# Two feed-forward sums opened early, one pair projected in four array tiles, and feed-forward units at equal distances, in a fused attention and feed-forward kernel

## The chip, the cores and the metric

One core of a Trainium2 chip (trn2). The metric is the device time of one execution in microseconds (us). The kernel before takes 306.46 us (median of 3 runs, 306.44 to 306.5). A profile has a span a little shorter than the run's time.

## The reference

Attention over 4 batches, 8 heads, 768 positions and 64 dimensions, in which a query sees only the keys whose six hash bits equal its own; then a feed-forward layer with a SiLU gate.

```python
q_bits = (einsum('bhsd,dk->bhsk', q, proj) > 0)           # the same for k
mask   = bucket(q_bits)[..., :, None] == bucket(k_bits)[..., None, :]
scores = where(mask, q @ k.T / sqrt(D), -1e9)
x = softmax(scores) @ v                                   # -> [3072, 512]
h = x @ w_in                                              # [3072, 2048]
out = (h / (1 + exp(-h))) @ w_out                         # [3072, 512]
```

## The kernel before

Two heads make a pair, two pairs are mostly prepared together. A pair's q and k are transposed (on TensorE for the first pairs, by stream transposes on VectorE for the later ones), projected on TensorE to hash bits, compared on VectorE, and the bits are copied beside the transposed q and k, so that one matmul gives score and mask together. The program is one list of 288 steps. A step is the value products of step w, then the score product and the exponential of step w + 3. What has to be ready later is planned for a step; feed-forward units are taken from a queue between steps.

```python
def t_unit(p, i):                       # four transposes into one PSUM bank, one copy out
    tp = ps.tile([P, 512], F32, tag="m", name="tp_ps", bufs=3)
    ...
    nc.vector.tensor_copy(out=qk32[p][:, 512 * i : 512 * (i + 1)], in_=tp)      # L187

def proj_unit(*pairs):
    for c0, w in ((0, 512), (512, S - 512)):
        bp = ps.tile([P, 512], F32, tag="m", name="bp_ps", bufs=3)
        for i, p in enumerate(pairs):
            for n in range(2):                        # q, k: one 32-column tile each
                c = 32 * (2 * i + n)
                nc.tensor.matmul(bp[c : c + 32, 0:w], pw[:, 0:32],              # L279
                                 qk32[p][:, n * S + c0 : n * S + c0 + w], ...)
    ...  # two comparisons on VectorE, L285

def bits_unit(pairs, i, par):           # two copies of 13 x 768 for each head
    for n in range(2):
        if n == 1 and par == 1:
            nc.vector.tensor_scalar(...)                                        # L307
        else:
            nc.vector.tensor_copy(out=dst, in_=bits[pairs][r, :])               # L310

def mm1(ci, grp):                       # one first or second sum of the feed-forward layer
    hp = ps.tile([P, f, n], F32, tag="m", name="h_ps", bufs=3)
    for j in range(f):
        for dt in range(NDT):                         # four K tiles, one for each pair
            nc.tensor.matmul(hp[:, j, :], w_in16[...], xT[4 * b + dt][...], ...)  # L423
    nc.scalar.activation(out=th, in_=hp, func=AF.Tanh, scale=0.5)               # L427
    after.append(...)                   # VectorE's gate from th and hp, L429

for w in range(NW):                     # cut: the planned work, the queue's filling
    flush()                             # gates of the step before
    for fn in at.pop(w, []): fn()
    n = -(-(len(moeq) - keep) // left) if len(moeq) > keep else 0
    skip = w % 3 == 2 or w % QST in (20, 21)          # no unit here
    ...
    for _ in range(n): moeq.popleft()()
    av(w)                                             # value products, L365
    score(w + LEAD)                                   # score product L333, exponential L336
```

All of `tp_ps`, `bp_ps`, `xt_ps` and `h_ps` rotate through the same three PSUM banks (tag "m").

The softmax here doesn't subtract the row's maximum and nothing guards it: scores larger than these inputs give would overflow.

## Time and profile before

| | before |
|---|---|
| time, median of 3 | 306.46 us |
| span of the profile | 304.1 us |
| TensorE, ScalarE, VectorE, GpSimd busy | 99%, 69%, 59%, 42% |
| first step to step 78 | ScalarE and TensorE near balance, units not yet begun |
| step 78 to about 135, and from 145 on | TensorE with almost no gaps (the largest 0.28 us) |

TensorE's busy share hides its waits, because its rows overlap (a unit's row is 1.03 us long, and the next row starts 0.86 us after it). The distance from one start to the next is what to read; the prediction does that with the lines it shows.

### The profile page before, as it was taken

Reading aid. Unit: us, or ns where it says so; the run is one execution under the profiler, and the core shown is the slowest. Engines: PE = TensorE matmul, PEld = TensorE weight load, DVE = VectorE, ACT = ScalarE, POOL = GpSimd, SP = SyncE. Lnnn points to the kernel's source line nnn. Section 1 sums busy time; section 2 is a strip of 40 time slices with the busy share of each in tenths; the row PEclk is TensorE's granted clock in tenths of the full one; section 3 lists DMA queues with packets and bytes.
Section 4 is the critical chain, followed back from the end, with each engine's and each line's share of the span. In section 5 each row is a group of like instructions: output and inputs, shape, how many; then the busy total and the mean of one; then the engine's idle time right before and its main releaser. Section 6 shows DMA issues by size and latency. Waiting matters only on the chain.

```text
span 304.1 us, 7165 instructions
## 1 busy us (share of the span) xinstructions
PE 299.6 (99%) x2710; PEld 174.9 (58%) x2710; DVE 180.7 (59%) x341; ACT 210.7 (69%) x392; POOL 129.2 (42%) x203
## 2 busy tenths in 40 slices
PE   8999999999999999999999999999999999999996
PEld 3675855555666545555565665555566654446653
DVE  5697977799559344854696334853543442664332
ACT  5987989988877696978976766878877732442300
POOL 7589999377506851855148321765111100000000
PEclk9999999999999999999999999999999999999999
DMA  7999898999979838854068246011022013001112
GB/s 204 242 241 195 179 149 127 226 160 99 165 133 187 137 77 237 127 113 133 2 115 125 76 63 197 5 42 32 2 60 63 0 38 95 34 2 69 37 63 75
DMA packets 102786, 32.87 MB, mean 108 GB/s; under 512 B 90656, under 2 KB 99808, under 8 KB 102752
## 3 DMA queue, kind: packets, MB, share of 16 engines
q1 hardware_dynamic: 98368, 28.22, 44.6%
q0 software_dynamic: 4224, 4.19, 9.1%
q8 instruction: 21, 0.34, 0.5%
q14 instruction: 13, 0.11, 0.1%
q10 hardware_dynamic: 160, 0.00, 0.0%
HBM read 27.27 MB, written 6.29 MB: 110 GB/s over the span
## 4 chain that ended last, share of the span: by engine, by line
PE 95%; DVE 3%; ACT 1%; issue 0%; POOL 0%; ACTq 0%; POOLq 0%
PE h_ps L423 26%; PE o_ps L455 26%; PE s_ps L333 20%; PE o_ps L365 13%; PE bp_ps L279 3%; PE tp_ps L185 2%; PE o_ps L441 1%; PE warm_ps L125 1%; DVE g L429 1%; DVE qka L310 1%; ACT u L336 1%; PE bp_ps L225 1%; PE tp_ps L198 1%; PE o_ps L356 0%; DVE bits L285 0%
## 5 line engine op out<-in xcount | busy, mean ns | idle before, releaser
L336 ACT ACTIVATE u<-s_ps 128x512 f16<-128x512 f32 x288 | 156.4, 602 | 39.9 <-PE s_ps L333 39.4
L429 DVE SCALAR_TENSOR_TENSOR g<-th,h_ps 128x512 f16<-128x512 f32 x96 | 65.1, 683 | 75.4 <-ACT th L427 75.4
L423 PE MATMUL h_ps<-xT,win 128*128 128x512 f16 (+1 forms) x512 | 97.4, 325 | 0.1
L365 PEld LDWEIGHTS <-u 128*128 128x128 f16 x1152 | 67.6, 98 | 42.9 <-ACT u L336 11.2
L455 PE MATMUL o_ps<-wout,g 128*128 128x512 f16 x368 | 91.6, 379 | 0.0
L365 PE MATMUL o_ps<-vv,u 128*128 128x65 f16 x1152 | 82.8, 194 | 0.3
L427 ACT ACTIVATE th<-h_ps 128x512 f32<-128x512 f32 x96 | 57.3, 597 | 36.6 <-PE h_ps L423 33.5
L423 PEld LDWEIGHTS <-win 128*128 128x128 f16 x512 | 49.9, 98 | 31.8 <-issue 0.4
L385 POOL TENSOR_TENSOR x_pr<-osum,rec 128x384 f16<-128x384 f32 x23 | 19.0, 826 | 89.4 <-DVE rec L384 89.0
L455 PEld LDWEIGHTS <-g 128*128 128x128 f16 x368 | 35.8, 98 | 34.1
L333 PE MATMUL s_ps<-qka 71*128 71x512 f16 x192 | 52.7, 327 | 0.2 <-DVE qka L238 0.2
L333 PE MATMUL s_ps<-qkb 128*128 128x512 f16 x192 | 52.8, 326 | 0.0
L251 POOL TENSOR_SCALAR qka<-qk 64x1536 f16<-64x1536 f32 x15 | 22.0, 1465 | 12.1 <-DVE qk L246 6.8
L460 DVE TENSOR_SCALAR osb<-o_ps 128x512 f32<-128x512 f32 x23 | 15.8, 686 | 15.5 <-PE o_ps L455 15.5
L251 POOL TENSOR_SCALAR qkb<-qk 64x1536 f16<-64x1536 f32 x15 | 22.1, 1471 | 1.2
L262 POOL TENSOR_TENSOR vsa<-v_sb 128x192 f32<-128x192 f32 x32 | 19.3, 604 | 0.0
L260 POOL CAST vv<-v_sb 128x384 f16<-128x384 f32 x32 | 16.7, 520 | 0.9 <-DMA v_sb<-in_v_dram 0.5
L333 PEld LDWEIGHTS <-qka 71*128 71x128 f16 x192 | 15.4, 97 | 0.8 <-ACT qka L238 0.6
L246 DVE STREAM_TRANSPOSE qk<-k_blk 128x768 f32<-128x768 f32 x10 | 15.8, 1576 | 0.0
L246 DVE STREAM_TRANSPOSE qk<-q_blk 128x768 f32<-128x768 f32 x10 | 15.7, 1572 | 0.0
L333 PEld LDWEIGHTS <-qkb 128*128 128x128 f16 x192 | 15.4, 97 | 0.0
L379 DVE TENSOR_TENSOR osum<-o_ps,vsum 128x390 f32<-128x390 f32 x23 | 13.0, 565 | 2.3
(64 smaller groups left out, 164.8 us busy)
## 6 DMA issues: line engine op xcount, KB each, us to landing
out_dram<-osb SPq DMA_DIRECT2D x23, 256.0 KB
v_sb<-in_v_dram SPq DMA_DIRECT2D x15, 384.0 KB
q_blk<-in_q_dram SPq DMA_DIRECT2D x40, 96.0 KB
k_blk<-in_k_dram SPq DMA_DIRECT2D x40, 96.0 KB
win<-in_moe_w_in_dram POOLq DMA_DIRECT2D x4, 512.0 KB, 8.1
wout<-in_moe_w_out_dram POOLq DMA_DIRECT2D x4, 512.0 KB, 8.1
q_sb<-in_q_dram SPq DMA_DIRECT2D x5, 384.0 KB
k_sb<-in_k_dram SPq DMA_DIRECT2D x5, 384.0 KB
```

The lines of the kernel that those rows point to most:

```text
L246: nc.vector.transpose(out=dst, in_=qk_sb[p, "qk"[n]])
L251: nc.gpsimd.tensor_scalar(out=dst[rows, :], in0=qk32[p][rows, :], scalar1=CS, scalar2=1.0, op0=ALU.mult, op1=ALU.mult)
L260: nc.gpsimd.tensor_copy(out=vv[:, :, 0:D], in_=src)
L262: nc.gpsimd.tensor_tensor(out=sa, in0=src[:, 0:3], in1=src[:, 3:6], op=ALU.add)
L333: nc.tensor.matmul(sp[:, o0 : o0 + n], t[rows, S + jt * P : S + (jt + 1) * P], t[rows, c0 : c0 + n], start=True, stop=True)
L336: nc.scalar.activation(out=u, in_=sp, func=AF.Exp, scale=ESC)
L365: nc.tensor.matmul(o_ps[h][:, c0 // P + i, :], u[:, o0 + i * P : o0 + (i + 1) * P], vv[:, jt, :], start=(not direct(h) and w % NU == 0 and ...
L385: (nc.vector if direct(h) else nc.gpsimd).tensor_tensor(out=x_pr[p][:, :, par * D : (par + 1) * D], in0=o[:, 0:NJ, 0:D], in1=rec[:, :, Non ...
L423: nc.tensor.matmul(hp[:, j, :], w_in16[:, dt, ft * P : (ft + 1) * P], xT[4 * b + dt][:, c0 : c0 + n], start=(dt == 0), stop=(dt == NDT - 1))
L427: nc.scalar.activation(out=th, in_=hp, func=AF.Tanh, scale=0.5)
L429: after.append(lambda: nc.vector.scalar_tensor_tensor(out=g[ci][:, grp * f : (grp + 1) * f, :], in0=th, scalar=1.0, in1=hp, op0=ALU.add, o ...
L455: nc.tensor.matmul(o2[tt], g[ci][:, ft, ct * P : (ct + 1) * P], w_out16[:, ft, :], start=(ft == 0), stop=(ft == NFT - 1))
```

## The change

Its intent is to fill TensorE's waits before step 78, to shorten one projection that blocks ScalarE, and to stretch batch 0's feed-forward units so that they don't run dry. Its core:

```diff
+    def proj_halves(p):                       # pair 1: four tiles of 384 columns
+        for c in range(4):
+            half, n = divmod(c, 2)
+            nc.tensor.matmul(bp[32 * c : 32 * c + 32, 0:HS], pw[:, 0:32],
+                             qk32[p][:, x0 : x0 + HS], start=True, stop=True)
+        nc.vector.tensor_scalar(...)          # one comparison of 128 x 384
+    def bits_halves(p, par):                  # four copies of 13 x 384 for each head
+        for c in range(4): ...
-    plan(10, lambda: proj_unit(1))
+    plan(10, lambda: proj_halves(1))
-        plan(11 + i, lambda i=i: bits_unit((1,), 0, i))
+        plan(11 + i, lambda i=i: bits_halves(1, i))
@@ the opened sums
+        if b == 0:
+            head = slice(0, NDT - 1)          # three of four K tiles
+            first = [mm1(0, 0, head), mm1(0, 1, head)] + [closing tiles] + first[2:]
+    for i in range(2):
+        plan(66 + 4 * i, first_units[0].pop(0))
-        plan(w0 + 20, lambda Q=Q: proj_unit(2 * Q, 2 * Q + 1))
+        wp = w0 + (24 if Q == 2 else 20)      # pairs 4 and 5: step 60, not 56
@@ equal distances
+        if BST + 5 <= w < 2 * BST:            # steps 77 to 143
+            skip = w * 36 // 66 == (w - 1) * 36 // 66
```

(The list of closures is written short here, and the lines that let `mm1` keep a sum open are left out; the cast of the 16-bit identity also moved from step 50 to the start.)

## The prediction

> **What bounds the kernel now.** I read the page first, then busy time by stretches of 10 us, then the waits of ScalarE, then the timelines of ScalarE and TensorE. I count the attention in steps: a step is four value products (128x65, line 365) followed by the score product of three steps later (128x512, or two of 128x256, line 333) and one exponential (line 336). There are 288 steps. Feed-forward units are inserted between steps: a unit is four 512-column matmuls, and batch 0 has 16 first sums, 8 second sums (these 24 have a tanh, line 427) and 12 output units in its list.
>
> ```profile
> PE 299.6 (99%) x2710; PEld 174.9 (58%) x2710; DVE 180.7 (59%) x341; ACT 210.7 (69%) x392; POOL 129.2 (42%) x203
> ...
> PE 95%; DVE 3%; ACT 1%; issue 0%; POOL 0%; ACTq 0%; POOLq 0%
> ```
>
> TensorE looks full, but matmul rows overlap each other, so 99% hides short waits. I therefore took the distance from one start to the next in TensorE's timeline. It is rigid: a unit 0.86 us, four value products 0.12, a score 0.22, a pair of projections (x16) 1.43. So a step costs TensorE 0.34 us; more than that is a wait. Two stretches of steps without units, then the start of the units:
>
> ```profile
> 48.73 0.30 PE L365 MATMUL o_ps<-vv,u 128*128 128x65 f16 x4
> 48.87 0.38 PE L333 MATMUL s_ps<-qkb 128*128 128x512 f16 x1
> 49.23 0.29 PE L365 MATMUL o_ps<-vv,u 128*128 128x65 f16 x4
> ...
> 53.50 1.03 PE L423 MATMUL h_ps<-xT,win 128*128 128x512 f16 x4
> 54.36 0.28 PE L365 MATMUL o_ps<-vv,u 128*128 128x65 f16 x4
> 54.48 0.38 PE L333 MATMUL s_ps<-qkb 128*128 128x512 f16 x1
> 54.70 1.03 PE L423 MATMUL h_ps<-xT,win 128*128 128x512 f16 x4
> ...
> 108.45 0.30 PE L365 MATMUL o_ps<-vv,u 128*128 128x65 f16 x4
> 108.58 0.38 PE L333 MATMUL s_ps<-qkb 128*128 128x256 f16 x2
> 108.94 0.30 PE L365 MATMUL o_ps<-vv,u 128*128 128x65 f16 x4
> ```
>
> Near 49 us a step takes 0.49-0.50 us, not 0.34: ScalarE's exponentials set the pace (28 in 14.39 us and 22 in 10.93 us, so 0.50-0.51 each). From 53.5 us (step 78) units follow with no gap: TensorE is the bound. Near 108 us a step takes 0.49 again: batch 0's list has run dry before the next one may start. From 113 us to the end I find no gap over 0.1 us. So only waits before 113 us can be removed. ScalarE's own stalls show the other thing to remove:
>
> ```profile
> 10.85 4.86 ACT L336 ACTIVATE u<-s_ps 128x512 f16<-128x512 f32 x9 [0.37 <-PE s_ps L333]
> 16.98 9.54 ACT L336 ACTIVATE u<-s_ps 128x512 f16<-128x512 f32 x18 [1.27 <-PE s_ps L333]
> 28.17 14.39 ACT L336 ACTIVATE u<-s_ps 128x512 f16<-128x512 f32 x28 [1.65 <-PE s_ps L333]
> 43.63 10.93 ACT L336 ACTIVATE u<-s_ps 128x512 f16<-128x512 f32 x22 [1.08 <-PE s_ps L333]
> ```
>
> Each stall of over 1 us is a projection on TensorE. Three scores stand ahead of ScalarE; the stall is about the inserted work less 0.47 us (1.43 gives 0.96, measured 1.08; a 0.33 us transposition gives none, and none is there).
>
> **What the Trainium skill says.** "TensorEngine Tiling (Array Packing)", Key Properties: tiles operate independently, so matmuls of different tiles run in parallel. The trace agrees: four fp32 matmuls of pair 1 in two tiles and eight of two pairs in four tiles both take 1.43 us. "Perfetto Trace Analysis", Identifying the Most-Contended Engine: matmul busy share is not a measure of distance from the limit; here 99% with some 5 us of gaps agrees. "SBUF — State Buffer", Who interferes with whom: a VectorE instruction in a two-port mode and GpSimd block each other for a whole instruction. The trace agrees: a masking of bits (13x768, line 307) takes 0.41 us at 29.69 us, and 1.54 at 18.61, beside a GpSimd cast that began at 18.48 and took 1.47.
>
> **Part 1, pair 1 in four tiles.**
>
> ```profile
> 14.94 1.49 PE L279 MATMUL bp_ps<-qk,pw 128*32 128x512 f32 x8
> 15.40 0.12 PEld L279 LDWEIGHTS bp_ps<-qk,pw 128*32 128x32 f32 x2 [0.31 <-issue]
> ```
>
> Before, each of two tiles passes 512 + 256 columns: 1.43 us. After, four tiles pass 384 each: half, 0.72 us (the first pair does just this on line 225, at 0.78 and 0.87 us with a wait behind). Saved: 0.7 us. From 10 to 25 us TensorE has next to no gaps, and ScalarE's 18 exponentials there run at 0.53, TensorE's pace; so the 0.7 us lies on the path, and the 1.27 us stall becomes about 0.6. On VectorE one comparison of 128x384 (0.68, line 228) replaces two (1.25), but eight copies replace four. Pair 1's first bits were ready at 18.20 us and used at 19.04; both move earlier alike. Gain **0.7 us**.
>
> **Part 2, the opened sums.** Three quarters of two units, 2 x 0.65 us of matmuls, move to steps 66 and 70, where TensorE waits about 0.15 us a step; the closing quarters (0.22 us each) come at steps 77 and 79. This is not simply 1.3 us gained: by step 81 both kernels have done the same matmuls, exponentials and two tanhs, and ScalarE is the bound there. By its chain: the exponential of step 80 began at 54.06 us. Earlier by 0.7 and later by two new stalls of 0.65 - 0.47 = 0.18, exponential 79 ends at 53.72. Then tanh, exponential 80 at 0.49 each end at 54.70; adding 0.16 for the signal and 0.34 for the step, step 81 begins on TensorE at 55.20. Before it began at 56.24. The difference is 1.04, of which 0.7 is part 1's: gain **0.34 us**. Moving the projection of pairs 4 and 5 from step 56 to 60 moves its stall, and lets the transposed input of pair 2 be ready for step 66; the cast of the identity to the start fills an idle VectorE. Nothing for either.
>
> **Part 3, equal distances.** Before, units went at two of three steps from 78 and were used up at about step 135. Ten steps remained at ScalarE's pace: the gaps from 107.99 to 112.07 us add to 1.26, with smaller ones about 1.3. After, 36 units over 66 steps, 0.55 a step, last to step 143. TensorE then needs 0.34 + 0.55 x 0.86 = 0.81 us a step; ScalarE, while every unit has a tanh, 0.49 x 1.55 = 0.76, later 0.6. TensorE stays the bound by a hair. Gain **1.3 us**. It is also where I expect a small loss: the rule no longer leaves out the steps beside the projection at step 92.
>
> Sum: 0.7 + 0.34 + 1.3 = 2.3 us. **Predicted 304.1 us**, 0.8% less.
>
> **Rivals.**
> (a) VectorE becomes the bound between steps 81 and 103. It was busy 9.83 of the 10 us from 60 to 70:
>
> ```profile
> 60.00:70.00 10.00, 10.00 (x95) 5.03 (x92) 9.83 (x17) 8.50 (x17) 8.35 (x8) 1.00 0.92 143
> ```
>
> Its four stream transposes (1.57 us each) are tied to steps 77 to 87, which now pass sooner; with gates and sums it has 10.1 us of work from step 81 to 92 and TensorE only 8.9. Its lag holds banks of the three-buffer tile, so units wait. Against: units 1.5 us apart leave slack of one or two banks. It would take back 0.3 to 1.2 us: 304.4 to 305.3.
> (b) The opened sums stall ScalarE more than 0.18 each, or the first closings wait for pair 3's input: part 2 gives zero, 304.4, or costs 0.5.
> (c) Everything before 53 us is late because of data: the DMA engines are nearly full there, so an earlier schedule meets the same landing times. Against: no wait of TensorE in the profile ends with a transfer after the start. It would eat part 1: 304.8.
> (d) The opened sums fill all 1.3 us and the stage after keeps the lead: 303.2. Against: ScalarE's chain above.
> (e) The smoothing merely moves the wait: unit against ScalarE at 0.81 to 0.76 leaves TensorE waiting at each step. Then part 3 gives half, 304.7.
>
> **Range and chances.** The parts are independent and each is bounded by a wait seen in the trace: at most 0.7, 1.3 and 1.5, so 303 is the floor. Rivals a and e are the likeliest losses, about 1 us together. Range 303.2 to 305.3. Two per cent is 6.1 us, more than all waits before 113 us: faster 0.01, within 2% 0.98, slower 0.01.
>
> **What would show it.** Right: the projection of pair 1 about 0.72 us from start to next start, ScalarE's stall behind it about 0.6; steps 66 and 70 with x3 matmuls of line 456 and ScalarE stalls under 0.3; the full third unit starting near 55.2 us; steps 135 to 144 without waits and with units; from step 155 on the same timeline, 2.3 us earlier. Wrong: TensorE waits over 0.2 us ahead of first sums between 56 and 78 us (rival a), or a step time near ScalarE's pace there (e), or waits for loads before 50 us (c), or a changed length of the stretch from step 155 to the end.

## The result, and the profile after

| | before | after |
|---|---|---|
| time, median of 4 | 306.45 us (305.86 to 306.5) | 305.72 us (305.5 to 306.25) |
| ratio after to before | | 0.9983 (95%: 0.9965 to 1.0001) |
| span of the profile | 304.1 us | 304.5 us |
| first score product starts at | 8.00 us | 8.82 us |
| score product issued in step 0 starts at | 9.20 us | 10.02 us |
| the one issued in step 145, counted from there | 104.57 us | 104.14 us |

A ratio is the mean time of one kernel's fast runs over that of the other's fast runs of the same rounds, so it is not quite the ratio of the medians. The time fell by about 0.7 us of the predicted 2.4 and lies outside the range; the interval of the ratio includes 1, so by time alone even this much is not certain.

The two profiles start 0.8 us apart, in code that neither kernel changed there, so I compare by a **ledger**: the start of the score product issued in a step, counted from the one issued in step 0. From step 145 to the end all kernels take the same time, within the span's rounding to 0.1 us. The ledger comes from one profile of each kernel. Where two kernels have the same code it agrees closely: at step 50 e2, e8, e9 and e11 stand between -0.33 and -0.36 us against the kernel before. By the ledger the change gains 0.43 us. The chain that ended last shows where it went; the first line is the page's busy line, the second the chain by engine.

```profile
PE 298.0 (98%) x2710; PEld 175.2 (58%) x2710; DVE 182.0 (60%) x344; ACT 210.2 (69%) x392; POOL 128.8 (42%) x203
...
PE 91%; DVE 6%; ACT 1%; issue 1%; POOL 0%; DVEq 0%; ACTq 0%; POOLq 0%
```

VectorE's share of the chain doubled, from 3% to 6%. TensorE's timeline after the change shows two new waits, in brackets at the end of a line, and the opened sums:

```profile
15.76 0.86 PE L298 MATMUL bp_ps<-qk,pw 128*32 128x384 f32 x8
16.55 0.30 PE L393 MATMUL o_ps<-vv,u 128*128 128x65 f16 x4
...
21.67 0.38 PE L361 MATMUL s_ps<-qka 71*128 71x512 f16 x1
23.03 0.66 PE L185 MATMUL tp_ps<-ident,q_sb 128*128 128x128 f32 x4 [0.98 <-DVE qk L187]
...
49.25 0.81 PE L456 MATMUL h_ps<-xT,win 128*128 128x512 f16 x3
49.90 0.28 PE L393 MATMUL o_ps<-vv,u 128*128 128x65 f16 x4
...
57.32 0.30 PE L393 MATMUL o_ps<-vv,u 128*128 128x65 f16 x4 [0.40 <-ACT u L364]
...
66.72 1.50 PE L279 MATMUL bp_ps<-qk,pw 128*32 128x512 f32 x16
68.82 1.02 PE L456 MATMUL h_ps<-xT,win 128*128 128x512 f16 x4 [0.60 <-DVE g L465]
```

The projection of pair 1 takes 0.79 us from start to next start (1.43 before). But at step 21 a transposition that should follow the score of 21.67 after 0.22 us starts 1.36 us after it: a wait of 1.14 us for VectorE's copy out of a PSUM bank. At step 92 a first sum waits 0.67 us (2.10 between the starts, less the projection's 1.43) for a gate on VectorE.

VectorE's timeline says why the first wait is there. After:

```profile
17.50 1.80 DVE L316 COPY qka<-bits 13x384 f16<-13x384 f16 x4
19.33 1.52 DVE L316 COPY qkb<-bits 13x384 f16<-13x384 f16 x1
20.86 0.55 DVE L313 TENSOR_SCALAR qkb<-bits,sc 13x384 f16<-13x384 f16 x1
21.43 0.55 DVE L316 COPY qkb<-bits 13x384 f16<-13x384 f16 x1
21.99 0.38 DVE L313 TENSOR_SCALAR qkb<-bits,sc 13x384 f16<-13x384 f16 x1
22.30 1.27 DVE L187 COPY qk<-tp_ps 128x512 f32<-128x512 f32 x2
```

And before:

```profile
17.46 0.74 DVE L310 COPY qka<-bits 13x768 f16<-13x768 f16 x2
18.24 0.36 DVE L310 COPY qkb<-bits 13x768 f16<-13x768 f16 x1
18.61 1.54 DVE L307 TENSOR_SCALAR qkb<-bits,sc 13x768 f16<-13x768 f16 x1
20.08 1.26 DVE L187 COPY qk<-tp_ps 128x512 f32<-128x512 f32 x2
```

Four bit copies took 2.69 us (17.46 to 20.15); eight take 4.87 (17.50 to 22.37), because a copy of half the columns is hardly shorter. The Trainium skill gives a reason: "VectorE: DVE Perf Modes", The TRN2 errata, states that VectorE pays a fixed extra time per instruction when it reads SBUF. Here a 13x768 copy takes 0.35 us at best, and a 13x384 one 0.37 at best in this profile (0.28 in e10), which agrees but does not show how much of it is fixed. The copies out of PSUM for pair 2 (line 187) stand behind them in VectorE's queue, and they free the banks for the next transpositions. The 1.52 us copy ran beside this GpSimd cast and ended 0.11 us after it; the kernel before had such a block too (1.54 us, in the lines above), without a wait on TensorE:

```profile
19.27 1.47 POOL L251 TENSOR_SCALAR qkb<-qk 64x1536 f16<-64x1536 f32 x1
```

ScalarE's stalls after, to set beside the four in the prediction:

```profile
17.16 5.87 ACT L364 ACTIVATE u<-s_ps 128x512 f16<-128x512 f32 x11 [0.64 <-PE s_ps L361]
24.12 3.78 ACT L364 ACTIVATE u<-s_ps 128x512 f16<-128x512 f32 x7 [1.08 <-PE s_ps L361]
29.55 8.76 ACT L364 ACTIVATE u<-s_ps 128x512 f16<-128x512 f32 x17 [1.65 <-PE s_ps L361]
...
47.27 3.04 ACT L364 ACTIVATE u<-s_ps 128x512 f16<-128x512 f32 x6 [1.11 <-PE s_ps L361]
50.49 2.06 ACT L364 ACTIVATE u<-s_ps 128x512 f16<-128x512 f32 x4 [0.18 <-PE s_ps L361]
52.74 3.54 ACT L364 ACTIVATE u<-s_ps 128x512 f16<-128x512 f32 x7 [0.19 <-PE s_ps L361]
```

The stall behind pair 1's projection fell from 1.27 to 0.64 as predicted. A new one of 1.08 us stands where TensorE waited at step 21, and the two of 0.18 and 0.19 are those of the opened sums.

### The profile page after: what moved, and what is told of

Read it like the earlier page. It is cut to its first block, busy times and chain, and to the rows that moved or that the text cites. A ratio compares the mean times of both kernels' runs of the same rounds, so it can differ in the third digit from the quotient of the medians.

```text
span 304.5 us, 7181 instructions
## 1 busy us (share of the span) xinstructions
PE 298.0 (98%) x2710; PEld 175.2 (58%) x2710; DVE 182.0 (60%) x344; ACT 210.2 (69%) x392; POOL 128.8 (42%) x203
## 4 chain that ended last, share of the span: by engine, by line
PE 91%; DVE 6%; ACT 1%; issue 1%; POOL 0%; DVEq 0%; ACTq 0%; POOLq 0%
PE o_ps L491 26%; PE h_ps L456 26%; PE s_ps L361 18%; PE o_ps L393 11%; PE bp_ps L279 3%; PE tp_ps L185 2%; DVE g L465 2%; PE o_ps L477 1%; ACT u L364 1%; PE warm_ps L125 1%; DVE qk L246 1%; PE bp_ps L225 1%; DVE qkb L316 1%; DVE qka L316 1%; PE tp_ps L198 1%
## 5 line engine op out<-in xcount | busy, mean ns | idle before, releaser
L463 ACT ACTIVATE th<-h_ps 128x512 f32<-128x512 f32 x96 | 58.0, 604 | 37.6 <-PE h_ps L456 34.9
```

## The experiments

Twelve kernels ran; all gave the right result, and all were timed in five rounds (the kernel before ran 11 times beside each group). "Ledger" is step 0 to step 145 against 104.57 us of the kernel before. The expectations speak instead of first score to end, which carries the span's rounding. e1 to e4 ran on one chip, e5 to e8 on a second, e9 and e10 on a third, e11 and e12 on a fourth; each ratio is against the kernel before on the same chip. No kernel is 2% faster than it, but all intervals except those of the change and of e4 lie below 1.

| kernel | pair 1 | opened sums | distances | else | median us | ratio (95%) | ledger |
|---|---|---|---|---|---|---|---|
| after | 4 tiles | yes | equal | | 305.72 | 0.9983 (0.9965-1.0001) | -0.43 |
| e1 | old | yes | equal | | 305.22 | 0.9963 (0.9949-0.9977) | -1.24 |
| e2 | 4 tiles, late copies | yes | equal | | 304.43 | 0.9945 (0.9933-0.9958) | -1.57 |
| e3 | old | no | equal | | 304.29 | 0.9940 (0.9928-0.9952) | -1.70 |
| e4 | old | yes | old | | 306.33 | 1.0005 (0.9992-1.0018) | +0.20 |
| e5 | 4 tiles | yes | equal | GpSimd cast later | 304.53 | 0.9943 (0.9927-0.9959) | -1.66 |
| e6 | as e2 | yes | equal | early transposes | 304.41 | 0.9944 (0.9930-0.9958) | -1.46 |
| e7 | as e2 | yes | equal but 92 | | 304.89 | 0.9963 (0.9948-0.9978) | -1.01 |
| e8 | as e2 | no | equal | | 304.18 | 0.9936 (0.9922-0.9950) | -2.02 |
| e9 | as e2 | yes | equal | VectorE relieved | 303.94 | 0.9927 (0.9914-0.9941) | -2.30 |
| e10 | as e2 | no | equal | cast later | 304.47 | 0.9949 (0.9936-0.9962) | -1.73 |
| e11 | as e2 | no | equal | VectorE relieved | 303.65 | 0.9916 (0.9895-0.9937) | -2.24 |
| e12 | as e2 | yes | equal | as e9, projection moved | 304.34 | 0.9933 (0.9913-0.9953) | -1.92 |

One of e9's runs was slow (309.19 us at a granted clock of 0.994) and is left out of its ratio. My theory after the first look: each part does what it was made for on TensorE, and VectorE takes it back, first through the order of its queue (steps 12 to 21), then through too much work (steps 77 to 100). The rivals: a phase effect against GpSimd, ScalarE's stalls, and the nearness of a unit to a projection.

### e1: the old projection of pair 1

```diff
-    plan(10, lambda: proj_halves(1))
+    plan(10, lambda: proj_unit(1))
-        plan(11 + i, lambda i=i: bits_halves(1, i))
+        plan(11 + i, lambda i=i: bits_unit((1,), 0, i))
```

> The changed kernel with pair 1 projected as before (two array tiles, two comparisons, four bit copies). Measured inside the profile from the first score product of step 0 to the end of the span, so that the varying start drops out: before 296.1 us, changed 295.7. Theory (the eight small bit copies keep VectorE for 4.9 us at step 11-12, pair 2's transposed data waits behind them in its queue, its PSUM buffer is not free, and TensorE waits 1.14 us at step 21): without them 0.64 us of projection comes back but the 1.14 and 0.26 us waits go, so 294.9 to 295.1, time about 0.7 us under the changed kernel. Rival (the wait at step 21 comes from the rest of the change or from the phase against GpSimd): the wait stays and the run is 0.6 us longer than the changed kernel, 296.3.

The wait at step 21 was gone, and the ledger 0.81 us shorter than with the four tiles. So part 1 as written **costs** 0.8 us: it saved 0.63, then lost 1.19 at step 21 (the wait of 1.14 and slower transpositions behind it) and 0.26 near step 46. First score to end was 294.8, just under the range I gave.

### e2: the second head's bit copies later

```diff
-        plan(11 + i, lambda i=i: bits_halves(1, i))
+        if i == 0:
+            plan(11, lambda: bits_halves(1, 0))
+    for c, wc in enumerate((13, 14, 16, 17)):
+        plan(wc, lambda c=c: bits_halves(1, 1, (c,)))
```

(`bits_halves` gets an argument that picks the copies.)

> The changed kernel with the four-tile projection kept, but the four bit copies of pair 1's second head (needed only at step 24) put one each at steps 13, 14, 16 and 17, behind pair 2's first transposed copy instead of all at step 12 ahead of it. Theory (order in VectorE's queue): the 1.14 us wait at step 21 goes, first score to end 294.3 to 294.7, 1.0 to 1.4 us under the changed kernel. Rival (VectorE has too much work there whatever the order, so the wait only moves): 295.5 or more, with a wait of about 1 us at another transposition before step 30.

The wait at step 21 is gone with all eight copies still there. VectorE's timeline shows pair 2's copies between them:

```profile
16.85 1.81 DVE L316 COPY qka<-bits 13x384 f16<-13x384 f16 x4
18.69 0.69 DVE L187 COPY qk<-tp_ps 128x512 f32<-128x512 f32 x1
19.41 0.80 DVE L316 COPY qkb<-bits 13x384 f16<-13x384 f16 x1
20.23 0.55 DVE L313 TENSOR_SCALAR qkb<-bits,sc 13x384 f16<-13x384 f16 x1
20.71 0.67 DVE L187 COPY qk<-tp_ps 128x512 f32<-128x512 f32 x1
```

The order in the queue is what mattered. Of the 0.63 us, 0.28 is lost again at step 28, where the projection of pairs 2 and 3 waits 0.66 us for such a copy (0.37 before). Part 1 then gains 0.33 (e2 against e1), not 0.7.

### e3: equal distances alone

```diff
+        if BST + 5 <= w < 2 * BST:
+            skip = w * 36 // 66 == (w - 1) * 36 // 66
```

> The kernel before with the equal distances alone (part 3). Theory: the idle of about 1.3 us at steps 135 to 144 goes, and up to 0.6 us comes back as a wait beside the projection at step 92: first score to end 296.1 - 1.3 + 0.3 to 0.6 = 295.1 to 295.4. Rival (ScalarE and TensorE are so balanced that waits move into the earlier steps): 295.8 to 296.1.

Part 3 alone gains 1.70 us, more than the change as a whole and more than expected (first score to end was 294.3). The unit beside the projection at step 92 waits only 0.15 us, and steps near the end of batch 0's list follow without a gap:

```profile
106.67 1.03 PE L455 MATMUL o_ps<-wout,g 128*128 128x512 f16 x4
107.54 0.28 PE L365 MATMUL o_ps<-vv,u 128*128 128x65 f16 x4
107.66 0.38 PE L333 MATMUL s_ps<-qkb 128*128 128x512 f16 x1
107.87 0.19 PE L360 MATMUL o_ps<-vs,dmat 128*128 128x65 f16 x1
107.90 0.29 PE L365 MATMUL o_ps<-vv,u 128*128 128x65 f16 x4
```

### e4: opened sums alone

The diff is e1's together with the equal distances taken out.

> The kernel before with the two opened sums, the moved projection of pairs 4 and 5 and the moved identity cast, but the old projection of pair 1 and the old distances (part 2 alone). Theory (ScalarE sets the pace up to step 81, so opening sums early gains only the rest): 0.2 to 0.4 us less than before, first score to end 295.7 to 295.9. Rival b (the two inserted pieces stall ScalarE as much as they save): 296.1 to 296.4. Rival d (the full 1.3 us is gained): 294.8.

Part 2 alone costs 0.20 us, by the ledger; the timed ratio, 1.0005, can't tell that from nothing. At step 81 it was 0.72 us ahead of the kernel before; by step 85 it had lost 0.94 us in one wait: a first sum behind the score of 59.55 us stood still until VectorE's gate had freed a bank, and that gate stood behind a stream transposition of 1.58 us in VectorE's queue. With the waits view of TensorE:

```profile
PE h_ps L456 <- DVE g L465: 0.8, 1, 0.8
```

Rival b of the prediction gave the right sign, but its reason (ScalarE's stalls) is not the larger part.

### e5: GpSimd's cast later

```diff
-    for i in range(2):
-        plan(8, lambda i=i: cast_unit(1, i))
-        plan(8, lambda i=i: v_unit(1, (i,)))
+    plan(8, lambda: cast_unit(1, 0))
+    for i in range(2):
+        plan(8, lambda i=i: v_unit(1, (i,)))
+    plan(8, lambda: cast_unit(1, 1))
```

> The changed kernel; only GpSimd's cast of pair 1's second head is put behind the value work of pair 1 instead of between it, so that it no longer runs while VectorE copies that head's bits (one of those copies took 1.52 us, 1.17 more than its neighbours, and ended as the cast ended). First score to end was 295.7 in the changed kernel. If the lock between the two engines is a needed part of the 1.14 us wait at step 21: the copies end about 1.1 us sooner and the wait is 0 to 0.2, 294.6 to 294.9. If the number of copies alone makes it (eight at 0.4 us): the wait stays over 0.8, 295.4 or more.

VectorE's timeline:

```profile
17.42 1.81 DVE L316 COPY qka<-bits 13x384 f16<-13x384 f16 x4
19.26 0.44 DVE L316 COPY qkb<-bits 13x384 f16<-13x384 f16 x1
19.72 0.55 DVE L313 TENSOR_SCALAR qkb<-bits,sc 13x384 f16<-13x384 f16 x1
20.28 0.39 DVE L316 COPY qkb<-bits 13x384 f16<-13x384 f16 x1
20.68 0.39 DVE L313 TENSOR_SCALAR qkb<-bits,sc 13x384 f16<-13x384 f16 x1
21.00 1.27 DVE L187 COPY qk<-tp_ps 128x512 f32<-128x512 f32 x2
```

The copy of 1.52 us takes 0.44 here, and the wait at step 21 is gone. The ledger, 0.42 shorter than e1's, now pays part of the 0.7. First score to end was 294.4, better than the range given. So the wait needed three things at once: twice the copies, the block by GpSimd, and the order. Taking away any one of them removed it.

### e6: VectorE's stream transposes earlier

```diff
-            w1 = w0 + (5, 9, 12, 15)[i]
+            w1 = w0 + ((3, 6, 9, 12) if Q == 3 else (5, 9, 12, 15))[i]
```

on top of e2.

> Experiment e2 (late copies, first score to end 294.4) with VectorE's four stream transposes of pairs 6 and 7 at steps 75, 78, 81, 84 instead of 77, 81, 84, 87. Theory (the opened sums make step 77 0.56 us later, VectorE starts its crowded stretch later and is still 0.7 us behind at step 92, where a feed-forward unit waits for the gate that frees its PSUM bank): the 0.68 us wait at step 92 goes, 293.7 to 293.9. Rival (the unit stands too near the projection, VectorE's backlog is not the cause): the wait stays, 294.3 to 294.5.

The wait at step 92 went, and two others came: 0.37 us at 60.1 and 0.41 at 72.2, together 0.78 for 0.68; first score to end was 294.6. The theory as I wrote it (a late start of the crowded stretch) fell; the rival fell too.

```profile
60.70 1.02 PE L456 MATMUL h_ps<-xT,win 128*128 128x512 f16 x4 [0.21 <-DVE g L465]
...
72.82 1.02 PE L456 MATMUL h_ps<-xT,win 128*128 128x512 f16 x4 [0.26 <-DVE g L465]
```

### e7: no unit at step 92

```diff
-            skip = w * 36 // 66 == (w - 1) * 36 // 66
+            skip = w * 36 // 66 == (w - 1) * 36 // 66 or w in (92, 93)
```

on top of e2.

> Experiment e2 with no feed-forward unit at steps 92 and 93, so that the unit that waited 0.68 us behind the projection comes at step 94. If nearness to the projection is what matters: the wait goes and nothing replaces it, 293.7 to 293.9. If VectorE is behind with its work: part of the wait comes back within a few steps, 294.1 to 294.4.

Again no wait at 92, but 0.86 us at 71.7 and 0.39 at 74.1, both ahead of a first sum; first score to end was 295.0, worse than either forecast. e6 and e7 fit a wait that is VectorE's work and only moves. Busy time by stretches (VectorE is the third engine) in the changed kernel:

```profile
61.00:65.00 4.00, 4.00 (x40) 2.36 (x39) 4.00 (x6) 4.00 (x9) 3.25 (x3) 1.00 1.25 206
65.00:69.00 4.00, 3.40 (x34) 1.43 (x32) 3.93 (x8) 2.71 (x6) 3.07 (x3) 1.00 0.86 129
69.00:73.00 4.00, 4.00 (x39) 2.27 (x38) 3.89 (x8) 3.12 (x6) 3.77 (x8) 1.00 0.75 98
```

This alone proves nothing: the same view of the kernel before reads 4.00, 3.88 and 3.86 for VectorE, with no wait of TensorE over 0.1 us in that time. Whether VectorE holds TensorE has to be tested by relieving it, which e9 does.

### e8: late copies and equal distances, no opened sums

The diff is e2's, with the opened sums and the move of the projection from step 56 to 60 taken out.

> Part 1 with late copies and part 3, without the opened sums and the moved projection. From the ledger of the first four (part 3 alone -1.70 us, part 1 with late copies -0.33, opened sums +0.45): first score to end 296.1 - 2.0 = 294.1, 0.3 under e2 and e3. If the opened sums did gain something beside part 1: 294.5 or more.

As expected, to 0.1 us: the ledger is 2.02 shorter than before. The opened sums cost 0.45 in this setting (e2 against e8), and 0.46 with the old projection (e1 against e3).

### e9: VectorE relieved

```diff
-            w1 = w0 + (5, 9, 12, 15)[i]
+            w1 = w0 + ((3, 7, 11, 15) if Q == 3 else (5, 9, 12, 15))[i]
-            plan(wp + (i if Q < 4 else 0),
+            plan(wp + ((0, 6, 12, 18)[i] if Q == 3 else i if Q < 4 else 0),
```

on top of e2.

> Experiment e2 (opened sums kept, late copies; first score to end 294.4) with VectorE's load between steps 77 and 100 thinned out: the four stream transposes of pairs 6 and 7 at steps 75, 79, 83, 87, and the bit copies of these pairs at steps 92, 98, 104 and 110 instead of 92 to 95. Theory (with the opened sums VectorE, 97 to 100% busy from 57 to 77 us, sets the pace there, and e6 and e7 could only move its wait): no wait of TensorE on a gate over 0.2 us is left, and the opened sums then give 0.1 to 0.2 us over e8: 293.7 to 294.0. Rival (the opened sums lose for another reason): the waits go but first score to end stays over 294.2, or the waits stay.

The waits view of TensorE has no VectorE gate left:

```profile
PE warm_ps L125 <- POOL warm L114: 1.0, 1, 1.0
PE o_ps L393 <- ACT u L364: 0.4, 1, 0.4
PE s_ps L361 <- DVE qka L238: 0.2, 1, 0.2
```

The unit behind the projection at step 92 now follows with no wait (1.43 us after the projection's start; 2.12 in e2), and the ledger is 0.73 shorter than e2's. This is what shows that VectorE held it. The ledger is 2.30 shorter than before. That this is nearly the predicted 2.34 is luck: e9 has two further edits, and e11 gets 2.24 without part 2.

### e10: late copies and late cast, no opened sums

The diff is e8 with e5's.

> Experiment e8 (late copies, equal distances, no opened sums; first score to end 294.0) with GpSimd's cast of pair 1's second head behind the value work as well. In e8 0.28 us of the 0.63 us of the projection is given back at the projection of pairs 2 and 3 (step 28), in e5 none there but 0.21 at step 46. If VectorE's queue is what gives it back, both together keep 0.4 to 0.63 us: 293.7 to 293.9. If not, 294.0 to 294.1 as in e8.

A miss: the projection at step 28 waited 0.92 us instead of 0.65, and the ledger is 0.29 longer than e8's. The cast did not stop blocking; it met another bit copy, which took 1.33 us at 20.48 beside a cast that began at 20.23 and took 1.47. Two remedies that each work do not add up here; likely each fitted only where the other engine then stood.

### e11: relieved, no opened sums

The diff is e9's with the opened sums and the moved projection taken out.

> Experiment e9 without the opened sums and the moved projection of pairs 4 and 5. It measures what the opened sums are worth once VectorE is relieved. If they are worth what the prediction gave them (0.34 us): first score to end 294.1, against 293.7 of e9. If the whole difference of e9 from e8 was VectorE's relief: 293.7.

The ledger is 2.24 shorter than before, against 2.30 of e9. With VectorE out of the way the opened sums are worth 0.06 us, which I can't tell from zero by time (303.65 against 303.94 on different chips). e11 has the lowest median of all.

### e12: the projection of pairs 2 and 3 at step 30

```diff
-    plan(28, lambda: proj_unit(2, 3))
+    plan(30, lambda: proj_unit(2, 3))
-        plan(29 + i, lambda i=i: bits_unit((2, 3), i // 2, i % 2))
+        plan(30 + i, lambda i=i: bits_unit((2, 3), i // 2, i % 2))
```

on top of e9.

> Experiment e9 with the projection of pairs 2 and 3 at step 30 instead of 28 and its bit copies one step later each. In e9 (as in e2, e6, e7, e8) that projection waits 0.65 us for VectorE's copy of pair 3's last transposed tile, which was made one step earlier; two more steps should cover it. Expected: wait under 0.2 us, first score to end 293.1 to 293.4, the best of all. If VectorE is the bound there too: the wait moves to the next transposition or to the bits of pair 2 (needed at step 33), 293.6 or more.

A miss as well: the wait at the projection went, and pair 2's bits came too late for the first score that needs them.

```profile
PE s_ps L361 <- DVE qka L338: 0.9, 1, 0.9
...
PE tp_ps L185 <- DVE qk L187: 0.3, 1, 0.3
```

The ledger is 0.38 longer than e9's. That projection stays where it was.

## Why the prediction was wrong

The sum was 0.7 + 0.34 + 1.3. The ledger gives, for the change as it was made: part 1 +0.81 (after against e1), part 2 +0.46 (e1 against e3), part 3 -1.70 (e3 against before), together -0.43. So part 1 missed by 1.5 us, part 2 by 0.8, and part 3 gave 0.4 more than forecast.

- **Part 1, the step that failed** is this sentence: "On VectorE one comparison of 128x384 (0.68, line 228) replaces two (1.25), but eight copies replace four. Pair 1's first bits were ready at 18.20 us and used at 19.04; both move earlier alike." It asked only whether the bits are ready for their own reader. It did not ask what stands behind the copies in VectorE's queue. The copies went from 2.69 to 4.87 us, and pair 2's copies out of PSUM, next in line, held three banks; TensorE waited 1.14 us (e1, e2, e5). TensorE's own saving was right: 0.64 us against 0.7 predicted (line 225 at 0.78 us was the better guide than half of 1.43), and ScalarE's stall 0.64 against "about 0.6".
- **Part 2, the stalls.** "two new stalls of 0.65 - 0.47 = 0.18". ScalarE's idle times were as forecast, 0.18 and 0.19, but they are not the loss. In the kernel before, exponentials start 0.48 us apart and take 0.60, so they overlap; over the stall of 0.18 the next one starts 0.82 us after the last, 0.34 later than it would. By the ledger, after against before, TensorE lost 0.28 at the first (steps 65 to 69), 0.29 at the second (69 to 73) and 0.08 more by step 77. (The chain also began at 54.06 us for an exponential that the trace has at 53.93.) With the opened sums step 81 came only 0.08 us earlier than without (e1 against e3, each from its own step 0), not 0.34.
- **Part 2, what followed** was worse and is rival (a). Doing matmuls of steps 77 to 81 earlier lets TensorE pass the stretch after it sooner, but the gates, transposes and bit copies of that stretch stay on VectorE, which is 95 to 100% busy from step 81 to step 100. It is as busy there in the kernel before, so its share alone would not have told; the likely reading is that TensorE now comes sooner to the bank that a gate has yet to free. The prediction named the 10.1 us of work against 8.9 and then charged nothing for it in the sum; "units 1.5 us apart leave slack of one or two banks" was wrong at step 92. The wait was 0.67 us, within the 0.3 to 1.2 given to that rival, and the sign named for it (over 0.2 us ahead of a first sum between 56 and 78 us) came. e9 against e2 shows the cause.
- **Part 3** was right in mechanism and too small: 1.70 instead of 1.3. In e3 the gaps at steps 135 to 144 are gone, and so is the wait of 0.24 us ahead of a first sum at 74.47 us in the kernel before, which the prediction left out. The two together are 1.5 to 1.6. e3 also gains 0.15 us by step 81, where its first unit comes a step earlier, and loses 0.14 beside the projection at step 92, the small loss that was expected; the last 0.1 I can't assign.
- **Rival (c)**, late data: the waits view shows no wait of TensorE that a transfer ends, in any run. **Rival (e)**, units against ScalarE: TensorE waited 0.57 us for an exponential once, at step 80, where ScalarE's chain had said it would, and not at each step. **Rival (d)** did not happen.
- **The range** rested on the phrase "The parts are independent". They were not: parts 1 and 2 both end at VectorE. With its queue reordered and its work moved apart, the three parts reach -2.30 (e9), of which part 2 is 0.06 (e11).

What stays open: the 0.26 us lost near step 46 in the changed kernel (a transposition waits for VectorE there, and two copies took 1.58 and 1.53 us; no experiment isolated it).

## What to carry to other kernels

When work on the bounding engine is shortened by cutting it finer, count the instructions that come out on the next engine and look at what stands behind them in that engine's queue, not only at their own reader. Moving work of the bounding engine earlier can be worth nothing (0.06 us at best here) if another engine, full in the stretch it leaves, must still do its share there: sum that engine's work over the stretch and charge the excess. And where instructions overlap, count a stall from start to start, not by the idle time. And smoothing alone can beat the bundle: here it gave 1.70 us, while the whole change gave 0.43.

## What the Trainium skill lacked or had wrong

- "TensorE: Matmul & The Clock Gate", Part 1, says that the array starts at half rate and that the window which releases it runs freely, so that the start varies between runs. The runs agree, and show what it does to this kernel: over 14 profiles the first score product came between 7.88 and 8.82 us after the span's start, up to 0.9 us apart, more than the change gained. In the six profiles in which the first matmuls of the first projection took 849 or 850 ns it came at 8.58 or later, in the other eight (509 to 689 ns) at 8.50 or earlier. It also advises to cross-check clock data; the granted clock in the page's stretches did not show it. The first pair's projections (line 225, durations as min/median/max in ns) in the changed kernel and, second fence, the kernel before:

```profile
L225 PE MATMUL bp_ps<-qk,pw x16: 486/667/849, 5.7 to 10.7; 128*32 128x384 f32 x16
...
5.00:7.00 2.00, 2.00 (x10) 0.20 (x8) 0.50 (x1) 1.76 (x4) 1.35 (x4) 1.00 0.84 244
```

```profile
L225 PE MATMUL bp_ps<-qk,pw x16: 486/498/511, 5.4 to 9.9; 128*32 128x384 f32 x16
```

  The same matmuls took up to 849 ns beside 486, while the granted clock of 5 to 7 us reads 1.00.
- "TensorEngine Tiling (Array Packing)", PSUM Bottleneck, warns that after a tiling speed-up the copy out of PSUM may become the bound. Here that copy became shorter (0.68 for 1.25 us); what became the bound was the distribution after it, four small copies for two, 0.37 us at best each in the changed kernel. No section of that page has this.
- "SBUF — State Buffer", Who interferes with whom, has the block between VectorE and GpSimd right (1.52 us beside a cast of 1.47). It does not say what e5 and e10 show: moving one instruction of the pair can free one wait (1.14 us) or only move the block to another copy (1.33 us).
